# Where the first-block row-maximum scores stand in a slot of a fused attention and MLP kernel

## The chip, the cores and the metric

The kernel runs on one core of a Trainium2 chip. The metric is the device time of one execution in microseconds (us); lower is better. All engines of the core take part: TensorE (PE, with its weight loads shown as PEld), VectorE (DVE), ScalarE (ACT), GpSimd (POOL), and SyncE (SP), which issues the DMAs.

## The reference

For `x` of 2048 tokens by 512 features, the kernel computes `x + s * g`. `s` is attention over the normalised `x` with 32 heads of 16 features, in which a query sees the 256 keys up to and including its own position. `g` is a gated MLP of the normalised `x` (hidden size 1792). Cut to what matters:

```python
def _A_ref(x, wqkv, wo):                 # H = 32 heads, Dh = 16, window W = 256
    q, k, v = ...                        # (x @ wqkv), by heads
    scores = einsum("bhqd,bhkd->bhqk", q, k) * (Dh ** -0.5)
    mask = (idx[:, None] - idx[None, :] >= 0) & (idx[:, None] - idx[None, :] < W)
    p = softmax(where(mask, scores, -1e9), axis=-1)
    return (p @ v, heads joined) @ wo

xn = layernorm(x)
s = _A_ref(xn, A_wqkv, A_wo)
g = silu(gelu(layernorm(xn) @ w1 + b1) @ w2 + b2)
return x + s * g
```

With query blocks of 128 rows, a window of 256 reaches over three key blocks: the query's own block, the one before it, and a part of the one two before. That last one is called the first block here.

## The kernel before

The heads are taken four at a time: 8 groups `n` of 16 query blocks `qb`, so the attention stage is a loop over 128 slots `t = 16 n + kb`. The order on each engine is the order of the program text. In a slot the kernel works on several query blocks at different stages:

- `prob_block(n, kb, p)` makes the scores of key block `kb` for two heads (pair `p`) with the keys as rows: one pair of matmuls, on the upper and the lower 64 rows of the array, into `stb`. ScalarE takes their exponential into a tile `pt`, and GpSimd masks the two end blocks of it. There is one buffer `stb`, of two PSUM banks, for both pairs: pair 1 is made at the start of the slot and pair 0 in its middle.
- `max_block(n, qb)` finds the row maxima for the slot that comes 12 later (`LEAD`). Four matmuls make the scores of the own and the previous key block into `xy`, and four more, for `qb >= 2`, make those of the first block into `zo[:, :, 0:256]`. VectorE then copies, under a mask, the first block's scores over those of the own block (a key is in the window in exactly one of the two), and reduces `xy` to the maxima `mt`. `xy` and `zo` have one buffer each.
- `pv_step(n, qb)` multiplies the probabilities `pt` of the previous slot by the values `vt`: up to 24 recorded matmuls of 17 columns, four column tiles side by side, into `otb = zo[:, 1, 256:384]`, which is in one of the two banks of `zo`. ScalarE copies the result into `oraw`.
- `fill_in(t, 0)` and `fill_in(t, 1)` put matmuls of other work (projections of later heads, the values, the first hidden layer) into the two halves of the slot. `tandem` plans most of them: two jobs run side by side, one on the upper and one on the lower 64 rows, into the two banks `fb`; in a second phase they change rows (a unit is one matmul of each).

From the loop at the end of `mixer_kernel` the order on TensorE in a slot is thus: `stb` of pair 1, `xy`, `zo` (first block), fills of the first half, `stb` of pair 0, fills of the second half, `zo` (values' products). The waits between engines are derived from the tiles that each instruction reads and writes. After the loop follow the MLP and the output projection.

All instructions are issued through a helper on line 42, so that every row of the profile names L42, and the tiles tell the rows apart.

Of the kernel before, what the change touches and what calls it, by code (L numbers as in the profile page):

```python
# [18 lines left out]
P = 128  # L19
# [6 lines left out]
NEG = -3.0e38  # L26
LEAD = 12
EARLY = 10


class Ordered:
# [18 lines left out]
def mixer_kernel(ctx, tc, x, wqk, wv, wo, w1, b1, w2, b2, out):  # L50


    nc = SimpleNamespace(**{name: Ordered(tc, name) for name in ("tensor", "vector", "scalar", "gpsimd", "sync")})
# [117 lines left out]
    big = bigp.tile([P, 2, KT, S], F32R, tag="big", name="xnT")  # L171
    x23 = bigp.tile([P, 9, 512], F32, tag="qk1", name="x_23")
    slots = []
# [5 lines left out]
    wva = bigp.tile([P, 2, KT, 256], F32R, tag="wa", name="wva")  # L179
    wqs = {}  # L180
# [10 lines left out]
    xy = psum.tile([P, 2, 512], F32, name="xy")  # L191
    zo = psum.tile([P, 2, 512], F32, name="zo")
    otb = zo[:, 1, 256:384]
    psf = attn.enter_context(tc.tile_pool(name="psf", bufs=1, space=PSUM))
    fb = [psf.tile([P, 512], F32, name=f"fb{i}") for i in range(2)]
# [164 lines left out]
    def pair_qk(n, c):  # L360

        ops = [(kt, a, b) for kt in range(KT) for a, b in PASSES]
        sl = slice(512 * c, 512 * (c + 1))

        def mm(ps, i, r, **flags):
            kt, a, b = ops[i]
            nc.tensor.matmul(ps, wqs[n][r, a, kt], big[r, b, kt, sl], **flags)

        def send(src, qk, tt):
            copy_rows(slots[n % 2][tt:P:4, qk, :, sl], src[64 * qk: 64 * qk + 64])  # L370

        def finish(ps, t, copy):
            hi = sgp.tile([P, 512], F32R, tag="sh", name=f"sh_{n}_{c}", bufs=2)
            raw = t2.tile([P, 512], F32, tag="t2", name=f"pjr_{n}_{c}")
            lo = raw.bitcast(F32R)
            copy(raw, ps)

            def send_high():
                if n >= 2:
                    copy_rows(slots[n % 2][3:P:32, 0, :, sl], slots[n % 2][7:P:32, 0, :, sl])  # L380
                for i, (qk, tt) in enumerate(((1, 0), (0, 0), (1, 2), (0, 1))):
                    send(hi, qk, tt)
                    if i == 1 and (n, c) in among:
                        among[n, c]()

            def send_low():
                send(lo, 1, 1)
                send(lo, 0, 2)


            free = t if (n, c) == (1, 2) else max(t + 1 + 2 * (c % 2), 16 * n - 28 + 4 * c)
            free += 2 * (t == 90)
            (behind if free == t else at)(free, nc.scalar.copy, hi, raw)
            behind(free, send_high)
            free = quiet(max(free, t + 1))
            at(free, lambda: nc.gpsimd.tensor_tensor(lo, raw, hi.bitcast(F32), op=ALU.subtract))
            behind(free, send_low)
        return 3 * KT, mm, finish

    def quiet(t):  # L400
# [9 lines left out]
    def pair_v(i):  # L410

        def mm(ps, k, r, **flags):
            j, kt, (a, b) = k // 12, k % 12 // 3, PASSES[k % 3]
            kb = 2 * i + j
            nc.tensor.matmul(ps[:, 256 * j: 256 * (j + 1)], big[r, a, kt, P * kb: P * (kb + 1)], wva[r, b, kt],
                             **flags)

        def finish(ps, t, copy):
            copy(vt[:, 2 * i: 2 * i + 2, :, 0:DH], ps.rearrange("p (b h d) -> p b h d", b=2, d=DH))
        return 6 * KT, mm, finish  # L420

    def pair_h(f):

        def mm(ps, k, r, **flags):
            kt, (a, b) = k // 3, PASSES[k % 3]
            nc.tensor.matmul(ps, w1_part(a, f)[r, P * kt: P * (kt + 1)], mlp["yy"][b][kt][r], **flags)

        def finish(ps, t, copy):
            raw = t2.tile([P, 512], F32, tag="t2", name=f"hr_{f}")
            copy(raw, ps)  # L430
            if f < 4:
                soon[f] = raw
            else:
                behind(t, nc.sync.dma_start, h_d[f - 6], raw)
        return 3 * KT, mm, finish
# [3 lines left out]
    def tandem(t0, t1, one, two, mid=None, back=None):  # L439

        n = one[0]
        lo, hi = slice(0, 64), slice(64, P)
        mid = mid or max(1, (t0 + t1 + 1) // 2)
        most = n // 4

        def places(slots, last):

            last = min(most, n // (len(slots) + 1)) if last else 0  # L450
            cuts = [(n - last) * k // len(slots) for k in range(len(slots) + 1)]
            out = []
            for t, a, b in zip(slots, cuts, cuts[1:]):
                ahead = min(b - a, max(most, (b - a + 1) // 2))
                out += [(t, 0)] * ahead + [(t, 1)] * (b - a - ahead)
            return out + [(t1, 0)] * last

        first, second = places(range(t0, mid), False), places(range(back or mid, t1), True)
        for phase, where in enumerate((first, second)):
            for i in range(n):  # L460
                flags = dict(start=(phase == 0 and i == 0), stop=(phase == 1 and i == n - 1), skip_group_check=True)
                def unit(i=i, phase=phase, flags=flags):
                    (two if phase == 0 else one)[1](fb[1 - phase], i, hi, **flags)
                    (one if phase == 0 else two)[1](fb[phase], i, lo, **flags)
                fills.setdefault(where[i], []).append((unit, ()))
        fills.setdefault((t1, int(t1 in BEHIND)), []).append((one[2], (fb[0], t1, nc.scalar.copy)))
        fills[t1, 0].append((two[2], (fb[1], t1, nc.vector.tensor_copy)))
# [12 lines left out]

    mts = {}

    def max_block(n, qb):

        slot = slots[n % 2]
        if qb % 4 == 0:
            mts[n, qb // 4] = small.tile([P, 2, 2, 4], F32, tag="mt", name=f"mt_{n}_{qb}")
        lo = max(qb - 1, 0)
        off = 128 * (lo + 1 - qb)

        def scores(p, a, first):
            r = slice(64 * a, 64 * a + 64)
            out, keys = ((zo[:, a, P * p: P * (p + 1)], slice(P * (qb - 2), P * (qb - 1))) if first else
                         (xy[:, a, 256 * p + off: 256 * (p + 1)], slice(P * lo, P * (qb + 1))))
            nc.tensor.matmul(out, slot[r, 0, p, P * qb: P * (qb + 1)], slot[r, 1, p, keys], start=True, stop=True)

        for p, a, first in ((0, 1, False), (0, 0, False), (1, 1, False), (1, 0, False),
                            (0, 1, True), (0, 0, True), (1, 1, True), (1, 0, True)):
            if qb >= 2 or not first:
                scores(p, a, first)  # L500
        four = xy.rearrange("q a (p k) -> q a p k", p=2)
        nc.vector.copy_predicated(four[:, :, :, 128:256], mask,
                                  neg if qb < 2 else zo[:, :, 0:256].rearrange("q a (p k) -> q a p k", p=2))
        nc.vector.tensor_reduce(out=mts[n, qb // 4][:, :, :, qb % 4],
                                in_=four[:, :, :, off:256],
                                axis=AX.X, op=ALU.max, negate=True)
# [51 lines left out]
    outs = {}  # L558

    def pv_step(n, qb):  # L560

        lo = max(qb - 2, 0)
        for kb in range(lo, qb + 1):
            for j in range(4):
                nc.tensor.matmul(otb[32 * j: 32 * j + DH + 1], vt[:, kb, (4 * n + j) % 16],
                                 pts[n, kb, j // 2][:, j % 2, P * (qb - kb): P * (qb - kb + 1)],
                                 start=(kb == lo), stop=(kb == qb),
                                 skip_group_check=True, tile_position=(0, 32 * j))
        if qb % 4 == 0:
            outs[0] = sgp.tile([P, 512], F32, tag="or", name=f"oraw_{n}_{qb}", bufs=2)  # L570
        nc.scalar.copy(outs[0][:, P * (qb % 4): P * (qb % 4 + 1)], otb)
        if qb % 4 == 3:
            (at if n or qb > 7 else behind)(16 * n + qb + 2, nc.sync.dma_start, oT_d[n // 2, n % 2::2, :, P * (qb - 3): P * (qb + 1)], outs[0])


    mlp = {}
# [23 lines left out]
    def w1_part(a, f):  # L600
        at = area(W1_AREA[f]) if f in W1_AREA else mlp["w1"]
        return at[:, 512 * a: 512 * (a + 1)]
# [63 lines left out]
    ahead = load(pp, "pt", x[512: 640, :], "x_1_0")  # L666
# [28 lines left out]
    n, raw = raws["qk"]  # L695
# [113 lines left out]
    end = 16 * NQ  # L809
    for t in range(-16, end + 1):  # L810
        m = t + LEAD
# [8 lines left out]
                    [P, 2, 512], F32, name="stb"))  # L820
            prob_block(t // 16, t % 16, 1)
        if t >= 0 and m < end:
            max_block(m // 16, m % 16)
        fill_in(t, 0)
        for fn, args in plan.get(t, []):
            fn(*args)
# [4 lines left out]
        fill_in(t, 1)  # L831
        if 0 <= m < 4:
            max_block(0, m)
        if t >= 1:
            pv_step((t - 1) // 16, (t - 1) % 16)
        run(lns.get(t, ()))
# [457 lines left out]
```

## Time and profile before

| | |
|---|---|
| median of 3 runs | 754.41 us (754.2 to 754.52) |
| span of the profiled execution, first to last instruction | 752.7 us |
| own time of the profiled execution beside its span | not given; the median is 1.7 us above the span |
| PE busy | 739.3 us (98%) |
| DVE busy | 512.6 us (68%) |
| ACT busy | 439.5 us (58%) |
| POOL busy | 300.6 us (40%) |
| slot loop, about 62 to 433 us | 128 slots |

A row of the timeline gives the start in us from the span's start, the duration, the engine, the line, the operation, the tile written and the tiles read, the shapes, and how many instructions are merged; in brackets stands the idle time of the engine before it and what ended that. Ends of matmuls are modelled, so a busy PE is not PE at its peak, while their starts are recorded. The granted TensorE clock was 0.999 of full speed over the span.

### The profile page before, as it was taken

The page shows a single profiled execution, that of the slowest core. Times are in us where ns is not written, and L with a number is a line of the kernel's source. Part 1 is how long each engine was busy: PE and PEld are TensorE (multiplying, and loading weights), DVE is VectorE, ACT ScalarE, POOL GpSimd, SP SyncE. Part 2 cuts the span into 40 slices and gives each one's busy share as a digit, 9 for nine tenths or more (in the row PEclk, how much of TensorE's full clock was granted, in tenths as well). Part 3 has the DMA queues.
Part 4 walks back from the last instruction along what each step waited for, and adds up shares of the span by engine and source line. Part 5 has one row for each costly group of instructions (what it writes and reads, how often), then busy time and mean ns, then how long its engine had stood idle before and what let it go on. Part 6 is the DMA issues. An engine that isn't in the chain of part 4 may idle for free.

```text
span 752.7 us, 18758 instructions
## 1 busy us (share of the span) xinstructions
PE 739.3 (98%) x7408; PEld 580.9 (77%) x7408; DVE 512.6 (68%) x781; ACT 439.5 (58%) x746; POOL 300.6 (40%) x644
## 2 busy tenths in 40 slices
PE   8999999999999999999999999999999999999997
PEld 7886676767778887676776688888888888888886
DVE  7886776877766778888772547863666765676643
ACT  7757767767666676778877845544553643442001
POOL 7414767757666555767867600120102000001102
PEclk9999999999999999999999999999999999999999
DMA  8633356766655525647725383542112232254621
GB/s 292 184 74 86 83 124 149 208 164 176 154 136 146 140 80 145 157 125 183 198 82 159 101 291 102 179 149 69 48 43 98 87 110 71 70 167 127 208 58 56
DMA packets 56951, 99.40 MB, mean 132 GB/s; under 512 B 11104, under 2 KB 11360, under 8 KB 56864
## 3 DMA queue, kind: packets, MB, share of 16 engines
q1 hardware_dynamic: 56864, 98.21, 45.7%
q8 instruction: 58, 0.95, 0.5%
q14 instruction: 29, 0.24, 0.1%
HBM read 51.39 MB, written 29.62 MB: 108 GB/s over the span
## 4 chain that ended last, share of the span: by engine, by line
PE 85%; ACT 5%; issue 5%; POOL 2%; DVE 1%; DMA 1%; SPq 0%; ACTq 0%; DVEq 0%; POOLq 0%
PE acc L42 20%; PE fb L42 17%; PE zo L42 12%; PE p L42 9%; PE stb L42 8%; PE s L42 6%; PE h L42 6%; PE xy L42 5%; ACT pt L42 3%; POOL pt L42 2%; PE pv L42 1%; PE yt L42 1%; ACT x L42 1%; DMA x<-in_x_dram 0%; DVE bnA L42 0%
## 5 line engine op out<-in xcount | busy, mean ns | idle before, releaser
L42 POOL TENSOR_SCALAR_AFFINE_SELECT pt<-pt 128x256 f32<-128x256 f32 x480 | 194.8, 430 | 134.0 <-ACT pt L42 132.7
L42 ACT ACTIVATE pt<-stb 128x768 f32<-128x768 f32 (+1 forms) x244 | 188.7, 773 | 55.0 <-PE stb L42 45.4
L42 DVE TENSOR_REDUCE mt<-xy 128x4 f32<-128x1024 f32 (+1 forms) x128 | 152.6, 1192 | 4.4
L42 DVE COPY_PREDICATED xy<-upper,zo 128x512 f32<-128x512 int32 x112 | 77.9, 696 | 75.0 <-PE zo L42 72.8
L42 PE MATMUL fb<-xnT,wqb 64*128 64x512 f32 (+1 forms) x684 | 115.0, 404 | 0.2
L42 POOL TENSOR_TENSOR xo<-xo,gated 128x512 f32<-128x512 f32 x15 | 20.3, 1356 | 216.5 <-DVE gated L42 213.2
L42 PE MATMUL zo<-pt,vt 128*17 128x128 f32 x2880 | 103.7, 275 | 0.5 <-POOL pt L42 0.3
L42 PE MATMUL stb<-qk 64*128 64x384 f32 (+1 forms) x488 | 96.4, 391 | 5.1 <-ACT pt L42 3.0
L42 PE MATMUL acc<-w,gh 128*128 128x512 f32 x320 | 98.9, 390 | 0.0
L42 PEld LDWEIGHTS zo<-pt,vt 128*17 128x17 f32 x2880 | 67.5, 97 | 36.7 <-issue 17.6
L42 PEld LDWEIGHTS stb<-qk 64*128 64x128 f32 x488 | 45.5, 183 | 50.4 <-ACT pt L42 40.6
L42 PEld LDWEIGHTS fb<-xnT,wqb 64*128 64x128 f32 (+1 forms) x684 | 63.8, 186 | 7.3 <-issue 0.6
L42 PEld LDWEIGHTS acc<-w,gh 128*128 128x128 f32 x320 | 59.8, 188 | 12.2
L42 PE MATMUL acc<-w,gl 128*128 128x512 f32 x160 | 62.4, 390 | 0.0
L42 PE MATMUL xy<-qk 64*128 64x256 f32 (+2 forms) x536 | 61.4, 302 | 0.5 <-DVE mt L42 0.4
L42 ACT COPY oraw<-zo 128x128 f32<-128x128 f32 x128 | 34.3, 268 | 38.8 <-PE zo L42 34.7
L42 PEld LDWEIGHTS xy<-qk 64*128 64x128 f32 x536 | 43.8, 185 | 9.7 <-DVE mt L42 2.9
L42 ACT ACTIVATE gated<-acc 128x512 f32<-128x512 f32 x16 | 8.7, 596 | 64.6 <-DVE acc L42 64.6
L42 PE MATMUL s<-wos,ohl 128*128 128x512 f32 (+1 forms) x204 | 44.7, 377 | 0.0
L42 PEld LDWEIGHTS s<-wos,ohl 128*128 128x128 f32 x204 | 36.7, 188 | 7.0
L42 ACT COPY p<-p 128x512 f32<-128x512 f32 x21 | 12.3, 585 | 49.5 <-PE p L42 42.2
L42 PE MATMUL zo<-qk 64*128 64x128 f32 x448 | 41.0, 260 | 0.0
(195 smaller groups left out, 1244.1 us busy)
## 6 DMA issues: line engine op xcount, KB each, us to landing
qk<-sh SPq DMA_DIRECT2D x128, 128.0 KB
qk<-pjr SPq DMA_DIRECT2D x64, 128.0 KB
oT_d<-oraw SPq DMA_DIRECT2D x32, 256.0 KB
w_d<-in_w_dram SPq DMA_DIRECT2D x14, 512.0 KB
x<-in_x_dram SPq DMA_DIRECT2D x16, 256.0 KB
or<-oT_d SPq DMA_DIRECT2D x16, 256.0 KB
w<-rden_d SPq DMA_DIRECT2D x16, 256.0 KB
xo<-in_x_dram SPq DMA_DIRECT2D x16, 256.0 KB
```

Source lines behind the costliest of these rows:

```text
L42: r = issue(*args, **kwargs)
```

## The change

In every slot from `t = 1` on, `max_block` leaves out the first-block scores of its query block (`ahead`). They are made one slot earlier instead, by a function of their own, `first_scores`, at the end of the slot: behind the fills of the second half and directly ahead of the values' products. So the four matmuls of block `m + 1` stand at the end of slot `t`, and the other four matmuls of that block, the predicated copy and the reduction stay at their places in slot `t + 1`. The fills keep their places. In addition, the first unit of a tandem's second phase gets a written dependency on ScalarE's latest copy into `oraw`; up to now the first-block scores stood between the two phases there.

```diff
+ORDER = mybir.DependencyInfo(mybir.DependencyClass.Sync, mybir.DependencyReason.DATA)
...
                 def unit(i=i, phase=phase, flags=flags):
-                    (two if phase == 0 else one)[1](fb[1 - phase], i, hi, **flags)
-                    (one if phase == 0 else two)[1](fb[phase], i, lo, **flags)
+                    made = ((two if phase == 0 else one)[1](fb[1 - phase], i, hi, **flags),
+                            (one if phase == 0 else two)[1](fb[phase], i, lo, **flags))
+                    if phase == 1 and i == 0:
+                        for r in made:
+                            tc.add_manual_dep(r.ins, outs["copy"].ins.name, ORDER, reason="the banks change rows")
...
-    def max_block(n, qb):
+    def first_scores(n, qb):
+
+        slot = slots[n % 2]
+        for p in range(2):
+            for a in (1, 0):
+                r = slice(64 * a, 64 * a + 64)
+                nc.tensor.matmul(zo[:, a, P * p: P * (p + 1)], slot[r, 0, p, P * qb: P * (qb + 1)],
+                                 slot[r, 1, p, P * (qb - 2): P * (qb - 1)], start=True, stop=True)
+
+    def max_block(n, qb, ahead=False):
...
+        if qb >= 2 and not ahead:
+            first_scores(n, qb)
...
-        nc.scalar.copy(outs[0][:, P * (qb % 4): P * (qb % 4 + 1)], otb)
+        outs["copy"] = nc.scalar.copy(outs[0][:, P * (qb % 4): P * (qb % 4 + 1)], otb)
...
         if t >= 0 and m < end:
-            max_block(m // 16, m % 16)
+            max_block(m // 16, m % 16, t > 0)
         fill_in(t, 0)
...
         fill_in(t, 1)
         if 0 <= m < 4:
             max_block(0, m)
+        if t >= 0 and m + 1 < end and (m + 1) % 16 >= 2:
+            first_scores((m + 1) // 16, (m + 1) % 16)
         if t >= 1:
             pv_step((t - 1) // 16, (t - 1) % 16)
```

The lines left out let the `mm` functions of the jobs return their matmul, which the dependency needs.

More of the change, by code (lines that the diff above doesn't have):

```diff
@@ L366, in mm @@
             kt, a, b = ops[i]
-            nc.tensor.matmul(ps, wqs[n][r, a, kt], big[r, b, kt, sl], **flags)
+            return nc.tensor.matmul(ps, wqs[n][r, a, kt], big[r, b, kt, sl], **flags)
         def send(src, qk, tt):
@@ L414, in mm @@
             kb = 2 * i + j
-            nc.tensor.matmul(ps[:, 256 * j: 256 * (j + 1)], big[r, a, kt, P * kb: P * (kb + 1)], wva[r, b, kt],
-                             **flags)
+            return nc.tensor.matmul(ps[:, 256 * j: 256 * (j + 1)], big[r, a, kt, P * kb: P * (kb + 1)],
+                                    wva[r, b, kt], **flags)
         def finish(ps, t, copy):
@@ L425, in mm @@
             kt, (a, b) = k // 3, PASSES[k % 3]
-            nc.tensor.matmul(ps, w1_part(a, f)[r, P * kt: P * (kt + 1)], mlp["yy"][b][kt][r], **flags)
+            return nc.tensor.matmul(ps, w1_part(a, f)[r, P * kt: P * (kt + 1)], mlp["yy"][b][kt][r], **flags)
         def finish(ps, t, copy):
@@ L489, in max_block @@
         off = 128 * (lo + 1 - qb)
[L491 to L500, printed above, removed]
+        for p in range(2):
+            for a in (1, 0):
+                r = slice(64 * a, 64 * a + 64)
+                nc.tensor.matmul(xy[:, a, 256 * p + off: 256 * (p + 1)], slot[r, 0, p, P * qb: P * (qb + 1)],
+                                 slot[r, 1, p, P * lo: P * (qb + 1)], start=True, stop=True)
+        if qb >= 2 and not ahead:
+            first_scores(n, qb)
         four = xy.rearrange("q a (p k) -> q a p k", p=2)
```

## The prediction

> **What bounds the kernel now.** I read the page first: where the time is and who carries the chain.
>
> ```profile
> span 752.7 us, 18758 instructions
> PE 85%; ACT 5%; issue 5%; POOL 2%; DVE 1%; DMA 1%; SPq 0%; ACTq 0%; DVEq 0%; POOLq 0%
> L42 PE MATMUL stb<-qk 64*128 64x384 f32 (+1 forms) x488 | 96.4, 391 | 5.1 <-ACT pt L42 3.0
> L42 PE MATMUL zo<-qk 64*128 64x128 f32 x448 | 41.0, 260 | 0.0
> ```
>
> TensorE (PE) carries 85% of the chain that ended last. The moved matmuls are the `zo<-qk` group: 448, four for each of 112 query blocks. The work after the attention stage runs on PE too, so what a slot gains or loses should reach the end. The busy column does not say whether PE is full, since the ends of its matmuls are modelled; I therefore use distances between starts. The chain cannot tell a PE that streams from one that has just been released either, so the waits of the slot loop came next (the view of who waited for whom, 62 to 400 us).
>
> ```profile
> DVE xy L42 <- PE zo L42: 68.3, 83, 1.5
> PEld stb L42 <- ACT pt L42: 40.4, 149, 0.9
> ```
>
> VectorE mostly waits for PE at the predicated copy; it is not the limit. PE's weight loads (PEld) wait for ScalarE's exponential at the scores `stb`, 149 times. There is one `stb` buffer: scores of pair 1, exponential, scores of pair 0, exponential, scores of pair 1. Each slot is thus two halves, and a half ends when the later of two is ready: PE with its own work, or the exponential that frees `stb`. This gate is what I need to measure. The timeline has two neighbouring slots that differ in the moved work: the slot at 357.95 treats a query block 1, which has no first-block scores; that at 360.75 a block 2, which has them.
>
> ```profile
> 357.95 0.44 PE L42 MATMUL stb<-qk 64*128 64x384 f32 x2
> 358.23 0.40 PE L42 MATMUL xy<-qk 64*128 64x256 f32 x4
> 358.47 0.85 PE L42 MATMUL fb<-xnT 64*128 64x512 f32 x6
> 358.50 0.81 ACT L42 ACTIVATE pt<-stb 128x768 f32<-128x768 f32 x1
> 359.36 0.19 PEld L42 LDWEIGHTS stb<-qk 64*128 64x128 f32 x2 [0.47 <-ACT pt L42]
> 359.37 0.44 PE L42 MATMUL stb<-qk 64*128 64x384 f32 x2
> 359.65 0.40 PE L42 MATMUL fb<-xnT 64*128 64x512 f32 x2
> 359.85 0.81 ACT L42 ACTIVATE pt<-stb 128x768 f32<-128x768 f32 x1
> 359.97 0.85 PE L42 MATMUL zo<-pt,vt 128*17 128x128 f32 x24
> 360.75 0.44 PE L42 MATMUL stb<-qk 64*128 64x384 f32 x2
> 360.89 0.27 ACT L42 COPY oraw<-zo 128x128 f32<-128x128 f32 x1 [0.23 <-PE zo L42]
> 361.03 0.40 PE L42 MATMUL xy<-qk 64*128 64x256 f32 x4
> 361.27 0.38 PE L42 MATMUL zo<-qk 64*128 64x128 f32 x4
> 361.32 0.81 ACT L42 ACTIVATE pt<-stb 128x768 f32<-128x768 f32 x1 [0.16 <-PE stb L42]
> 361.49 0.45 PE L42 MATMUL fb<-yh,xnT 64*128 64x512 f32 x2
> 361.75 0.70 DVE L42 COPY_PREDICATED xy<-upper,zo 128x512 f32<-128x512 int32 x1 [1.06 <-PE zo L42]
> 361.77 0.41 PE L42 MATMUL fb<-xnT 64*128 64x512 f32 x2
> 362.00 0.41 PE L42 MATMUL fb<-yh,xnT 64*128 64x512 f32 x2
> 362.23 0.40 PE L42 MATMUL stb<-qk 64*128 64x384 f32 x2
> 362.47 0.40 PE L42 MATMUL fb<-yh,xnT 64*128 64x512 f32 x2
> 362.67 0.81 ACT L42 ACTIVATE pt<-stb 128x768 f32<-128x768 f32 x1
> 362.79 0.85 PE L42 MATMUL zo<-pt,vt 128*17 128x128 f32 x24
> 363.57 0.44 PE L42 MATMUL stb<-qk 64*128 64x384 f32 x2
> ```
>
> (Start, duration, engine. `x2` is one pair of matmuls, side by side on the upper and lower 64 rows.) The second slot's first half takes 362.23 - 360.75 = 1.48 us. Its exponential ended at 361.32 + 0.81 = 362.13, and `stb` follows an exponential by 0.05 (358.50 + 0.81 = 359.31, then 359.36), so ScalarE would have allowed 362.18, a half of 1.43: PE was late by 0.05 and sets this half. Its second half, 1.34 us, is PE's as well: the exponential ended at 362.67 + 0.81 = 363.48, 0.09 before the next `stb`. In the first slot, without the four matmuls, PE was ready early and stood: its first half is 359.37 - 357.95 = 1.42 us, gated by ScalarE. So both engines are nearly in balance, and the two halves are limited separately.
>
> **The change part by part.** *Taking the four out of the first half.* With them, `xy` to the first `fb` takes 361.49 - 361.03 = 0.46; without, 358.47 - 358.23 = 0.24. The pair right behind them is slowed too: 361.49 to 361.77 is 0.28, against 0.23 for the next (361.77 to 362.00). Together 0.22 + 0.05 = 0.27 us of PE time. PE's own part of the half falls from 1.48 to 1.21. But the half itself cannot: the slot at 357.95 is exactly this first half without the four, and it took 1.42. So a common slot gains 0.06, and PE stands for the other 0.2.
>
> *Restart.* A `stb` pair that stood at the gate costs a little behind it as well: `stb` to `fb` 359.37 to 359.65 = 0.28, against 362.23 to 362.47 = 0.24 when PE came late. I take 0.045 on the second half wherever the stall is new.
>
> *Putting the four into the second half.* No row shows scores directly ahead of the values' products (`zo<-pt,vt`), so I build it. Before: `fb` to the products 362.47 to 362.79 = 0.32. After: `fb` to first scores as to a next pair, 0.23; the first pair of the four to the second 0.11 (half of 361.27 to 361.49); the second to the products unknown. Lower value: a 512-column pair takes 0.23 to the next pair and 0.32 to the products; at 0.23/512 = 0.45 ns a column a 128-column pair is 0.17 shorter, so 0.15. Upper value from `stb`, in two more slots:
>
> ```profile
> 368.11 0.39 PE L42 MATMUL stb<-qk 64*128 64x384 f32 x2
> 368.42 0.85 PE L42 MATMUL zo<-pt,vt 128*17 128x128 f32 x24
> 368.54 0.81 ACT L42 ACTIVATE pt<-stb 128x768 f32<-128x768 f32 x1 [0.53 <-PE stb L42]
> 369.40 0.44 PE L42 MATMUL stb<-qk 64*128 64x384 f32 x2
> 383.86 0.39 PE L42 MATMUL stb<-qk 64*128 64x256 f32 x2
> 384.37 0.60 ACT L42 ACTIVATE pt<-stb 128x512 f32<-128x512 f32 x1
> 385.33 0.28 PE L42 MATMUL stb<-qk 64*128 64x256 f32 x2
> 385.60 0.85 PE L42 MATMUL zo<-pt,vt 128*17 128x128 f32 x24
> ```
>
> 384 columns to the products 0.31, 256 columns 0.27, so 128 columns 0.23. The price is then 0.23 + 0.11 + (0.15 to 0.23) - 0.32 = 0.17 to 0.25. A pair that cost only its columns (2 x 128 x 0.45 = 0.12) is the floor. I take 0.18, near the value from `fb`, since an `fb` pair stands ahead of the four in most slots; 0.13 and 0.24 give the range. Below nothing is excluded: no PE work disappears.
>
> *Waits.* The four now need the predicated copy of the same slot (VectorE) to have read `zo`. That copy ended at 361.75 + 0.70 = 362.45; without the four ahead of it, it ends about 0.22 earlier, at 362.2 or so, while the four come at about 362.47 + 0.23 - 0.06 + 0.04 = 362.7. So the wait should cost nothing in the common slot. If the cover went, the products, the copy to `oraw` and the next `stb` would queue behind it on PE. The added wait, the first unit of a tandem's second phase on the copy to `oraw`, comes 22 times: that copy ends at 360.89 + 0.27 = 361.16, and the unit comes at 361.27 now that `zo` is gone. Nothing, with at most 22 x 0.1 = 2 us if the 0.11 of cover vanished. On VectorE the row maxima finish earlier; nobody on the chain is late for them. No DMA and no queue of SP or POOL is passed.
>
> *The sum.* I walked the `stb` rows of all slots in which one side of the move falls, 114 slots, and sorted them by the distance from an exponential's end to the next `stb` (0.05: gated; more: PE's). First and last of these slots begin at
>
> ```profile
> 64.91 0.44 PE L42 MATMUL stb<-qk 64*128 64x384 f32 x2
> 395.99 0.45 PE L42 MATMUL stb<-qk 64*128 64x384 f32 x2 [0.33 <-ACT pt L42]
> ```
>
> - 50 like that at 360.75, PE's at both ends: first half -0.07 on the mean, second 0.18 + 0.045. Net +0.153 each: +7.7.
> - 8 the same, but with a first half that stands 0.2 or more over its gate: -0.22 + 0.22: 0.
> - 16 whose second half is gated, like 368.11 to 369.40, 1.29 us with the exponential ending at 369.35: the four fall into PE's stall; -0.06 + 0.06: -0.1 in all.
> - 7 that only gain them (first half unchanged, as at 357.95): +0.15 each: +1.1. 7 that only lose them: -0.3. 7 with neither: 0.
> - 19 with short exponentials or a long first half, like 383.86: gate at 384.37 + 0.60 + 0.05 = 385.02, half ended 385.33. Here PE's part shrinks freely: -0.25 + 0.14 = -0.11 each: -2.1.
>
> Sum +6.3 us. The profiled execution's span is 752.7; its launch is not in the view, and the median of the runs, 754.41, is 1.7 above the span, which I carry over: 752.7 + 1.7 + 6.3 = 760.7. With 0.13 for the four the sum is +2.2, with 0.24 it is +11.2.
>
> **The rivals.** *Faster: the four hide ahead of the products.* From `fb` to the products PE takes 0.32 where a next pair takes 0.23, so there is a hole of 0.09 in each slot. If the four filled it and their second pair overlapped, their price would be near nothing: 50 x (-0.07 + 0.045) = -1.3, the 16 give -1.0, the 8 give -1.4, the 19 give -4.8, the 7 give -0.3; -8.8, so 745.6 us. It decides from a price of about 0.10 us downwards. For it: the stalls at the second gate (368.54 + 0.81, PE waiting from about 369.2) are real. Against it: the hole lies behind the last matmul whatever that is, and moves with it rather than being filled.
>
> *No change: the four cost only their columns, on both sides.* By 0.45 ns a column they are 0.12 in either half, and no restart is paid: 50 x (-0.07 + 0.12) = +2.5, 7 x 0.12 = +0.8, the 16 and the 7 about -1.5, the others 0: about +1.5, so 755.9 or a little less. Against it stands the measured 0.27. The Trainium skill's page "TensorE: Matmul & The Clock Gate", section "Back-to-back issue gap", has a rule of this kind: a matmul follows the last by its columns at 2.4 GHz plus 2.5 ns. By that rule two pairs of 128 columns would be 0.11 us wherever they stand, and the sum would be about +1. The trace disagrees where the four stand now, with 0.27 for the two pairs; it shows no row for the new place.
>
> *Slower still: VectorE becomes the bound.* If the predicated copy came later than the four by 0.15 in every slot, the products would wait behind them: 101 moved blocks x 0.15 = +15 more, 776. It decides once the copy ends over 0.5 us later than I place it (362.2 against 362.7), which the rows do not suggest.
>
> That the change does not do what it says is not likely: each engine keeps the program's order.
>
> **How the numbers follow.** About 0.2% (1.5 us) is what a measurement of this kernel can tell from no change. Forecast 0.60 (own range 756.6 to 765.6); hidden 0.15; columns only 0.14, of which 0.02 ends faster, 0.09 within and 0.03 slower; VectorE 0.06; something else that costs 0.05. That makes 0.17 faster, 0.09 the same, 0.74 slower. The range from 752.0 to 768.0 leaves out the hidden case and most of the VectorE case.
>
> **What would show it.** Right: first halves of common slots at 1.42 with `stb` 0.05 behind the exponential and PEld's wait for ScalarE well above 40.4 us; second halves near 1.55; the predicated copy, now 0.72 behind the first `xy` pair (361.03 to 361.75), at about 0.50. Wrong: second halves that hardly grow (the four are hidden), or first scores that start right behind the end of the predicated copy (VectorE), or first halves under 1.40 with an exponential of 0.81.

## The result, and the profile after

The changed kernel takes 765.59 us (764.86 to 766.09), the kernel before 754.39 us: slower by 11.2 us, ratio 1.0147 with a 95% interval of 1.0133 to 1.0161. The profiled spans, 763.9 and 752.7 us, differ by the same 11.2. Since the medians of the kernel before lie between 754.2 and 754.8 from one chip to the next, each experiment below is given by its distance from the kernel before measured beside it; the changed kernel stands at +11.2.

The page after, with those of its rows that answer to the ones shown of before (a new line at the top of the file makes L42 into L43; the moved `zo<-qk` matmuls no longer have a row of their own there):

```profile
span 763.9 us, 18757 instructions
PE 87%; ACT 5%; DVE 3%; DMA 2%; issue 2%; POOL 0%; SPq 0%; ACTq 0%; DVEq 0%
L43 PE MATMUL stb<-qk 64*128 64x384 f32 (+1 forms) x488 | 103.1, 418 | 4.4 <-ACT pt L43 1.1
```

The scores `stb` read 418 ns on the mean instead of 391. These ends are modelled, but the rise fits the next view, by which more of them start behind a wait, 172 instead of 149. Who waited for whom in the slot loop, 62 to 411 us:

```profile
DVE xy L43 <- PE xy L43: 88.9, 95, 2.1
PEld stb L43 <- ACT pt L43: 57.7, 172, 0.5
PEld zo L43 <- DVE xy L43: 0.9, 3, 0.4
```

TensorE's wait for the exponential rose from 40.4 to 57.7 us. VectorE's predicated copy is released by `xy` now, and TensorE hardly ever waits for that copy. This idle time of weight loads counts some that runs beside matmuls, so the size comes from starts again: by the distance of a `stb` from the `fb` matmul ahead of it, over the 0.235 us of an unhindered one, TensorE stood about 14.4 us at the first gate (2.0 before), and behind the values' products, over 0.21, about 2.1 us at the second (6.5 before). The common slot, the one that began at 360.75 before, in the timeline:

```profile
369.88 0.45 PE L43 MATMUL stb<-qk 64*128 64x384 f32 x2
370.16 0.40 PE L43 MATMUL xy<-qk 64*128 64x256 f32 x4
370.40 0.44 PE L43 MATMUL fb<-yh,xnT 64*128 64x512 f32 x2
370.45 0.81 ACT L43 ACTIVATE pt<-stb 128x768 f32<-128x768 f32 x1 [0.16 <-POOL pjr L43]
370.66 0.70 DVE L43 COPY_PREDICATED xy<-upper,zo 128x512 f32<-128x512 int32 x1 [1.01 <-PE xy L43]
370.90 0.41 PE L43 MATMUL fb<-yh,xnT 64*128 64x512 f32 x2
371.31 0.19 PEld L43 LDWEIGHTS stb<-qk 64*128 64x128 f32 x2 [0.45 <-ACT pt L43]
371.31 0.44 PE L43 MATMUL stb<-qk 64*128 64x384 f32 x2
371.59 0.39 PE L43 MATMUL fb<-yh,xnT 64*128 64x512 f32 x2
371.82 0.34 PE L43 MATMUL zo<-qk 64*128 64x128 f32 x4
372.09 0.85 PE L43 MATMUL zo<-pt,vt 128*17 128x128 f32 x24
372.87 0.46 PE L43 MATMUL stb<-qk 64*128 64x384 f32 x2
```

The first half is 371.31 - 369.88 = 1.43 us instead of 1.48. `stb` comes 0.05 behind the exponential (370.45 + 0.81 = 371.26), and the last `fb` pair began 0.41 ahead of it where 0.23 would do: 0.18 us of standing. The second half is 1.56 instead of 1.34: the four and the way to the products take 372.09 - 371.59 = 0.50 where `fb` to the products took 0.32, and `stb` to `fb` takes 0.28 instead of 0.24. The predicated copy begins 0.50 behind the first `xy` pair, as predicted, and ended at 371.36, 0.46 ahead of the four. So the slot takes 2.99 us for 2.82.

### The profile page after: what moved, and what is told of

Its sections match the earlier page's. It is cut to its first block, busy times and chain, and to the rows that moved or that the text cites. A ratio compares the mean times of both kernels' runs of the same rounds, so it can differ in the third digit from the quotient of the medians.

```text
span 763.9 us, 18757 instructions
## 1 busy us (share of the span) xinstructions
PE 748.9 (98%) x7408; PEld 587.6 (77%) x7408; DVE 511.2 (67%) x781; ACT 440.3 (58%) x746; POOL 300.4 (39%) x644
## 4 chain that ended last, share of the span: by engine, by line
PE 87%; ACT 5%; DVE 3%; DMA 2%; issue 2%; POOL 0%; SPq 0%; ACTq 0%; DVEq 0%
PE acc L43 20%; PE fb L43 16%; PE zo L43 13%; PE stb L43 10%; PE p L43 9%; PE s L43 6%; PE h L43 6%; ACT pt L43 4%; PE xy L43 4%; PE pv L43 3%; DMA qk<-qk 2%; DVE xy L43 1%; PE yt L43 1%; DMA x<-in_x_dram 1%; DVE mt L43 1%
## 5 line engine op out<-in xcount | busy, mean ns | idle before, releaser
L43 POOL TENSOR_SCALAR_AFFINE_SELECT pt<-pt 128x256 f32<-128x256 f32 x480 | 194.8, 430 | 146.1 <-ACT pt L43 144.7
L43 ACT ACTIVATE pt<-stb 128x768 f32<-128x768 f32 (+1 forms) x244 | 188.6, 773 | 50.4 <-PE stb L43 39.6
L43 DVE TENSOR_REDUCE mt<-xy 128x4 f32<-128x1024 f32 (+1 forms) x128 | 152.6, 1192 | 4.4
L43 DVE COPY_PREDICATED xy<-upper,zo 128x512 f32<-128x512 int32 x112 | 77.9, 695 | 84.4 <-PE xy L43 77.1
L43 PE MATMUL fb<-xnT,wqb 64*128 64x512 f32 (+1 forms) x684 | 112.9, 398 | 0.2
L43 PE MATMUL stb<-qk 64*128 64x384 f32 (+1 forms) x488 | 103.1, 418 | 4.4 <-ACT pt L43 1.1
L43 POOL TENSOR_TENSOR xo<-xo,gated 128x512 f32<-128x512 f32 x15 | 20.3, 1356 | 216.6 <-DVE gated L43 213.1
L43 PE MATMUL zo<-pt,vt 128*17 128x128 f32 x2880 | 103.7, 275 | 0.1
L43 PE MATMUL acc<-w,gh 128*128 128x512 f32 x320 | 98.9, 390 | 0.0
L43 PEld LDWEIGHTS stb<-qk 64*128 64x128 f32 x488 | 45.5, 183 | 68.7 <-ACT pt L43 57.7
L43 PEld LDWEIGHTS zo<-pt,vt 128*17 128x17 f32 x2880 | 67.5, 97 | 15.7 <-issue 7.0
L43 PEld LDWEIGHTS fb<-xnT,wqb 64*128 64x128 f32 (+1 forms) x684 | 63.8, 185 | 7.8 <-DVE pjr L43 1.1
L43 PEld LDWEIGHTS acc<-w,gh 128*128 128x128 f32 x320 | 59.8, 188 | 12.1
L43 ACT COPY oraw<-zo 128x128 f32<-128x128 f32 x128 | 34.3, 268 | 56.7 <-PE zo L43 53.5
L43 PE MATMUL acc<-w,gl 128*128 128x512 f32 x160 | 62.4, 390 | 0.0
L43 PE MATMUL xy<-qk 64*128 64x256 f32 (+2 forms) x536 | 58.0, 290 | 0.3 <-DVE mt L43 0.2
L43 PEld LDWEIGHTS xy<-qk 64*128 64x128 f32 x536 | 47.0, 185 | 6.4 <-issue 2.8
L43 ACT ACTIVATE gated<-acc 128x512 f32<-128x512 f32 x16 | 8.7, 596 | 64.5 <-DVE acc L43 64.5
L43 PEld LDWEIGHTS zo<-qk 64*128 64x128 f32 x448 | 39.2, 185 | 7.8 <-issue 1.4
L43 PE MATMUL s<-wos,ohl 128*128 128x512 f32 (+1 forms) x204 | 44.7, 377 | 0.0
L43 PEld LDWEIGHTS s<-wos,ohl 128*128 128x128 f32 x204 | 36.6, 188 | 7.0
L43 ACT COPY p<-p 128x512 f32<-128x512 f32 x21 | 12.3, 585 | 49.5 <-PE p L43 42.0
```

The source lines that it names most:

```text
L43: r = issue(*args, **kwargs)
```

## The experiments

Two theories were set against each other. The first: the two halves are gated separately, the move leaves TensorE standing in the first half and lengthens the second, and the loss is one of balance. The second: the four cost more at their new place as such, or VectorE comes in. Two smaller causes were taken from the trace of after, the written dependency and one DMA.

**Moving other work the opposite way.**

```diff
-                ahead = min(b - a, max(most, (b - a + 1) // 2))
+                ahead = min(b - a, max(most, (b - a + 1) // 2) + n // 12)
```

This puts one more unit of a tandem's fills (two of the shorter ones) into the first half of a slot. In the changed kernel:

> The changed kernel with one more unit of the tandems' fills (0.23 us of TensorE) in the first half of each slot and one less in the second, where the second half has one. Theory (TensorE stands about 0.2 us at the first gate and the second half is TensorE's): first halves 1.44 instead of 1.42, second halves 1.33 instead of 1.56, so about -0.2 us in some 75 slots: 748 to 752, below the kernel before. Rival (the loss is a price of the four at their new place, or VectorE's, and not an imbalance of the halves): 762 to 767.

Measured 752.33 us, -2.5 against the kernel before (ratio 0.9967, 0.9955 to 0.9980), 13.7 less than the changed kernel. The same slot in its timeline:

```profile
358.36 0.44 PE L43 MATMUL stb<-qk 64*128 64x384 f32 x2
359.35 0.64 PE L43 MATMUL fb<-yh,xnT 64*128 64x512 f32 x4
359.82 0.42 PE L43 MATMUL stb<-qk 64*128 64x384 f32 x2
360.08 0.34 PE L43 MATMUL zo<-qk 64*128 64x128 f32 x4
361.15 0.44 PE L43 MATMUL stb<-qk 64*128 64x384 f32 x2
```

Its halves are 1.46 and 1.33, 2.79 in all. With four `fb` pairs (two of them stand between the rows shown, at 358.88 and 359.13) the first half is nearly full, and the second has no fill left. In the kernel before:

> The same shift of one unit in the kernel before. Theory: first halves 1.48 + 0.23 = 1.71, second halves fall only to their gate of 1.28 to 1.35, about +0.17 in some 75 slots: about 766. Rival (the shift of the fills is a gain by itself, whatever the place of the four): below 754.

Measured 759.29 us, +4.5 (1.0059, 1.0044 to 1.0074).

```profile
365.21 0.45 PE L42 MATMUL stb<-qk 64*128 64x384 f32 x2
366.88 0.33 PE L42 MATMUL stb<-qk 64*128 64x384 f32 x2
367.26 0.81 ACT L42 ACTIVATE pt<-stb 128x768 f32<-128x768 f32 x1 [0.16 <-PE stb L42]
368.12 0.44 PE L42 MATMUL stb<-qk 64*128 64x384 f32 x2
```

First half 1.67, second 1.24. The direction is the theory's: the shift of the fills is a loss without the move and a gain with it. The size is not: I had expected about +12. The first halves grew by about 0.2 us in 85 slots, nearly as expected, but the second halves fell by 0.14 on the mean and not by 0.06. One reason is in the rows: I had taken a gate of 1.28 to 1.35 from slots where `stb` had waited. Behind a `stb` that comes late itself the exponential starts after 0.38 us (366.88 to 367.26), behind one that had waited after 0.48 (359.37 to 359.85, before), and the gate is then 1.24. The other is that second halves with more fills had more to give, 0.23 to 0.33 in 30 of the 85 slots.

**Loosening the gate.**

```diff
-        nc.scalar.activation(pt[:, :, 0:w], both[:, :, 0:w], AF.Exp, scale=DH ** -0.5)
+        nc.scalar.activation(pt[:, :, 0:min(w, 256)], both[:, :, 0:min(w, 256)], AF.Exp, scale=DH ** -0.5)
...
-            nc.gpsimd.affine_select(out=pt[:, :, 256:384], ...)
+            nc.gpsimd.memset(pt[:, :, 256:384], 0.0)
```

In the changed kernel:

> The changed kernel with the exponential on 256 of 384 columns (0.60 instead of 0.81 us); the probabilities of the third query block are set to zero by GpSimd instead, so this part of the attention is left out. Theory (ScalarE's exponential gates the first half): the gate falls from 1.42 to 1.21, where TensorE is ready, and the restart of 0.05 goes too: 0.2 to 0.25 us in some 75 slots, about 747 to 751. Rival (the four cost what they cost by their place on TensorE): over 760.

Measured 747.68 us, -7.2 (0.9914, 0.9898 to 0.9931): 18.4 less than the changed kernel. The first halves of the prediction's 50 common slots fell from 1.43 to 1.22 at the median. In the kernel before:

> The kernel before with the exponential on 256 of 384 columns; the probabilities of the third query block are set to zero by GpSimd, so that part of the attention is left out. Theory (with the gates loose only TensorE's own time is left, and there the four cost 0.27 us in the first half and 0.21 at the new place): the old order now loses against the new one, by 0.06 us in about 85 slots, so this kernel is 3 to 6 us slower than the changed kernel with the same short exponential (747.7), 751 to 753. Rival (the new order is dearer by its place, gates or not): faster than 747.7, about 740 to 745.

Measured 748.90 us, -5.3 (0.9933, 0.9918 to 0.9948). The waits of the two, the new order first:

```profile
PEld stb L43 <- ACT pt L43: 22.2, 89, 0.4
PEld stb L42 <- ACT pt L42: 12.5, 40, 0.7
```

With the long exponential the new order loses 11.2 us; with the short one it is ahead, by 1.85 us as the medians stand, at the edge of what two chips tell apart. So by itself the new order is not dearer on TensorE; what it loses with the long exponential, it loses in the main at the gate. (The edit also gives GpSimd a cheaper instruction, in both kernels; no run separates that from the shorter exponential.)

The 3 to 6 us that I had expected were not reached, and the starts in the two traces say why. In the 50 common slots the new order's first halves are 0.26 us shorter at the median, close to the 0.27 of the four, but its second halves are 0.26 longer, where I had put 0.21. Of these, 0.09 is the way from `stb` to `fb` (0.27 instead of 0.18): even with the short exponential, `stb` of the new order still comes right behind it in 20 of the 50 slots, so the restart had not gone. In the common slots the two orders are thus about equal; the small lead comes from other slots, and which cause makes it is open.

**Another place in the second half.** The four ahead of the fills instead of behind them:

```diff
+        if t >= 0 and m + 1 < end and (m + 1) % 16 >= 2:
+            first_scores((m + 1) // 16, (m + 1) % 16)
         fill_in(t, 1)
```

> The changed kernel with the four scores at the start of the second half, ahead of its fills, instead of directly ahead of the values' products. Theory (the price of short pairs is the weight loads around them: 0.11 + 0.11 and 0.05 on the pair behind, 0.27 as in the old first half): second halves 1.61 instead of 1.56 where they have fills, 2 to 5 us slower than the changed kernel, 767 to 770. Rival (the price comes from standing next to the products: 0.20 from the four to them): 760 to 764.

Measured 769.84 us, +15.6 (1.0207, 1.0193 to 1.0221), 4.4 more than the changed kernel. A second half of it:

```profile
371.52 0.44 PE L43 MATMUL stb<-qk 64*128 64x384 f32 x2
371.80 0.33 PE L43 MATMUL zo<-qk 64*128 64x128 f32 x4
371.97 0.45 PE L43 MATMUL fb<-xnT 64*128 64x512 f32 x2
372.35 0.85 PE L43 MATMUL zo<-pt,vt 128*17 128x128 f32 x24
373.13 0.44 PE L43 MATMUL stb<-qk 64*128 64x384 f32 x2
```

The half is 1.61. The four take 371.97 - 371.80 = 0.17 to the `fb` pair, and that pair then takes 0.38 to the products instead of 0.32: 0.23 in this slot, and second halves 0.05 longer than in the changed kernel in nearly all slots that have fills there. Directly ahead of the products is the cheaper place of the two; the price is paid around the short pairs, and on the long pair behind them.

**The written dependency.** Only for slots below 116:

```diff
-                    if phase == 1 and i == 0:
+                    if phase == 1 and i == 0 and where[0][0] < 16 * NQ - LEAD:
```

> The changed kernel with the written dependency on the copy to oraw only where first-block scores are still made (slots before 116); the two last tandems have none, as before the change. Theory (this wait costs 0.67 and about 0.4 us of idle weight loading at its two last places, because nothing stands between pair 1's scores and the first unit there): 0.8 to 1.0 us less than the changed kernel, about 764.7. Rival (the wait is hidden by the exponential behind it): no difference, 765.6.

Measured 763.83 us, +9.0 (1.0120, 1.0105 to 1.0135), 2.2 less than the changed kernel. In the changed kernel the unit waits for the copy to `oraw`:

```profile
419.31 0.44 PE L43 MATMUL xy<-qk 64*128 64x384 f32 x2
419.85 0.27 ACT L43 COPY oraw<-zo 128x128 f32<-128x128 f32 x1
420.17 0.19 PEld L43 LDWEIGHTS fb<-yh,xnT 64*128 64x128 f32 x2 [0.67 <-ACT oraw L43]
```

Without it, the same unit in this run:

```profile
418.08 0.44 PE L43 MATMUL xy<-qk 64*128 64x384 f32 x2
418.35 0.40 PE L43 MATMUL fb<-yh,xnT 64*128 64x512 f32 x2
```

0.27 behind the scores instead of 0.86. In the two last tandems, past the last first-block scores, nothing stands between pair 1's scores and the unit, and the copy to `oraw` can only follow an exponential. That is worth about 1 us: from slot 115 to the end this profile is 0.97 shorter than that of the changed kernel. Of the rest of the 2.2, 0.7 to 0.8 us is the next cause, which differs from profile to profile, and 0.5 lies ahead of the slot loop, where nothing was changed.

**One block left at its place.** Block 8 of head group 1, the first of its chunk, with the old order:

> The changed kernel with one block less moved: block 8 of head group 1 has its first-block scores at the old place, one slot later. Theory (there alone the four waited for a DMA of the projected queries that landed at 98.38 us, 0.1 us ahead of them): 1.0 to 1.3 us less than the changed kernel, about 764.4. Rival (the wait only moves to the other scores of that block, 1.3 us later in the order): under 0.4 us less.

Measured 764.27 us, +10.1 (1.0131, 1.0116 to 1.0147), 1.1 less. In the changed kernel's timeline the four of this block stand out:

```profile
97.07 1.23 DVE L43 TENSOR_REDUCE mt<-xy 128x4 f32<-128x1024 f32 x1
97.25 0.40 PE L43 MATMUL fb<-xnT,wqb 64*128 64x512 f32 x2
98.44 0.33 PEld L43 LDWEIGHTS zo<-qk 64*128 64x128 f32 x4 [1.18 <-DVE mt L43]
98.84 0.85 PE L43 MATMUL zo<-pt,vt 128*17 128x128 f32 x24
```

The row blames the reduction, whose end at 98.30 happens to lie near. But the four read nothing of it; the trace's semaphore record has the second DMA of the low parts of these queries (`qk<-pjr`, issued from 93.47 on) landing at 98.38. With the block at its old place the half ended 1.28 us earlier and the wait was gone, so the DMA is what the earlier place ran into. In the profile without the late dependency the same DMA lands at 97.09, and the four's weight load starts at 97.15: the wait moves with the landing.

**All of it together.** The shifted fills, the dependency below slot 116, and the four blocks of slots 1, 2, 11 and 91 at the old place:

> The changed kernel with one more unit of fills in the first half of each slot, the written dependency only below slot 116, and four blocks left at the old place (those of slots 1, 2, 11 and 91, where the move lost 0.24 to 1.4 us). Theory (the three causes are apart and add up): 1.0 for the dependency and 1.3 to 2.3 for the blocks below the kernel with the fills alone (752.3), 749 to 750, the fastest so far. Rival (the gain of the shifted fills was all there is): 751.5 to 752.5.

Measured 749.27 us (749.18 to 749.74), -4.9 (0.9936, 0.9923 to 0.9948): faster than both kernels and 2.4 further from the kernel before than the fills alone.

```profile
PEld stb L44 <- ACT pt L44: 44.5, 159, 0.7
```

The wait for the exponential (L44, since this kernel has one more new line) is near the 40.4 us of before again. What the dependency and the four blocks add on top of the fills was not measured apart.

## Why the prediction was right or wrong, point by point

- *Direction and mechanism: right.* The first half stopped at the gate (1.43 in the slot shown, 1.40 to 1.45 in 47 of the 50 common slots), and the second grew. The slot without the four in the trace of before had shown it, and the short exponential confirms the gate.
- *The price of the four in the second half, 0.18: right in size, partly by luck.* 0.50 - 0.32 = 0.18 in the slot shown. But two of its parts were off and cancel. In a narrow window (372.05 to 372.085) the timeline shows the second pair of the four alone:

```profile
371.88 0.28 PE L43 MATMUL zo<-qk 64*128 64x128 f32 x2
```

  It starts 0.06 behind the first pair, where I had put 0.11, and the products follow it after 0.21, where the 0.18 rested on 0.15. With 0.11 and 0.21 my sum would have been 0.23.
- *Restart, 0.045: right in the slot shown, too small on the whole.* 0.28 - 0.24 = 0.04 there. At the median of the 50 common slots `stb` to `fb` rose from 0.21 to 0.28, by 0.07. Their second halves grew by 0.24 on the mean, for 0.225 predicted.
- *The 50 common slots: too low, the largest miss of a term.* +9.9 us for +7.7. Without the slots at 95.56 (the DMA) and 89.37 they lost 0.171 each, for 0.153: +0.8. The slot at 89.37 gave 0.3 more; the DMA 1.1.
- *"Here TensorE's part shrinks freely", the 19 slots: right on the mean for the first halves, wrong for the second.* -0.7 for -2.1. The first halves fell by 0.27 each, for 0.25. The second halves grew by 0.24 each, for 0.14; the prediction names no rows from which it took 0.14. In three of the slots the first half did not shrink freely either, by 0.08 and not 0.25. They begin a tandem, and their first `fb` cannot start before the copies that empty the two banks of the last one:

```profile
108.42 0.68 DVE L43 COPY pjr<-fb 128x512 f32<-128x512 f32 x1
108.61 0.45 PE L43 MATMUL xy<-qk 64*128 64x256 f32 x4
109.16 0.53 PEld L43 LDWEIGHTS fb<-xnT,wqb 64*128 64x128 f32 x6 [0.29 <-DVE pjr L43]
```

  Before, the four had filled the time of that copy; the rows of before are these.

```profile
105.57 0.68 DVE L42 COPY pjr<-fb 128x512 f32<-128x512 f32 x1
106.05 0.34 PE L42 MATMUL zo<-qk 64*128 64x128 f32 x4
106.30 0.53 PEld L42 LDWEIGHTS fb<-xnT,wqb 64*128 64x128 f32 x6
```

  A cover that I had not looked for was taken away with them, about 0.5 us in the three slots. No run tested this row by itself.
- *The dependency, "nothing, at most 2 us": the bound held, the value did not.* I had looked at it where the copy to `oraw` comes early (cover 0.11), not in the last slots, where `xy` and the four no longer stand ahead of the unit. About 1 us.
- *"The wait should cost nothing" for the four: right for VectorE, and incomplete.* I had asked what the four wait for on VectorE and that no DMA is passed, but not when their operands land. A block read one slot earlier met its DMA: about 1.1 us in this profile.
- *The sum.* The 114 slots lost 10.0 us for 6.3: 2.2 of the difference lies in the 50, 1.4 in the 19, 0.5 in the 8 with a long first half, and the other groups together were 0.4 better than forecast. Outside them 1.2 was lost. Of this 0.4 is ahead of the first of them: 0.2 in slot 0, which has the four twice, and 0.2 before the slot loop, whose start differs by up to 0.5 between the profiles. The other 0.8 is from 398.81 on. My count had left out slot 0 and the slot at 398.81, where one side of the move falls too. That makes 11.2 for 6.3. The measured time is at the upper end of my own range, but not for the reason that I had given that end, a price of 0.24 for the four.
- *Rivals.* The hidden case and the VectorE case are out: the four were not hidden, and VectorE ended 0.46 ahead of them. Columns only falls too: it would give 0.12 for the two pairs, and the new place now shows 0.18, the place ahead of the fills 0.23. The formula that I named from the Trainium skill's page "TensorE: Matmul & The Clock Gate", section "Back-to-back issue gap", is given there for an isolated matmul, and the section itself says that it under-counts at small column counts when weight loads and matmuls alternate; I had left that out. These two measured prices, against an estimate of 0.11 by the formula, agree with that warning.

## What to carry to other kernels

Where one buffer passes back and forth between two engines, look at each half of the turn by itself: work taken out of a half buys nothing beyond the gate (here 0.07 us of 0.27), and the half that receives it pays in full. A move of this kind belongs together with a counter-move of the same size, and its worth is that of the pair (here +11.2 alone, +4.5 for the counter-move alone, -2.5 for both). Before reading something earlier, ask when its DMA lands, and what copy the moved work had been covering.

## What the runs showed of the hardware that was not expected

Two 128-column pairs ahead of a long pair delay what follows that one: 0.28 us from it to the next pair instead of 0.23 in the kernel before, and 0.38 instead of 0.32 to the products in the kernel with the four ahead of the fills. And behind a `stb` pair that had waited for the exponential, the next work starts later than behind one that came late itself: the next `fb` pair after 0.28 us instead of 0.18 to 0.24, the exponential after 0.48 instead of 0.38, so that the next gate moves from 1.24 to 1.28 and more.
